# One kernel, the same pieces of work: another hand-fixed order, and other engines where a piece may choose

## The chip, the cores and the metric

The kernel runs on one core of one Trainium2 chip. A core has five instruction streams: PE (TensorE: matrix multiplications and transposes through the array), DVE (VectorE), ACT (ScalarE), POOL (GpSimd) and SP (SyncE, which here only issues DMAs). Each stream runs its instructions strictly in the order in which the program gives them; across streams only semaphores order things. The metric is the device time of one execution in microseconds (us), and the median of several runs is compared.

## The reference

Pooled attention (8 batches, 8 heads, 576 queries, 72 pooled keys) feeds a block with a rotation, a mixing over tokens and a gated channel layer:

```
k_p, v_p = mean of k, v over groups of 8 tokens          # 576 -> 72
attn     = softmax(q @ k_p.T / sqrt(64))
x        = (attn @ v_p), heads side by side              # [8, 576, 512]
theta    = x @ w_theta
zr, zi   = x * cos(theta), x * sin(theta)
y        = w_tok_r @ zr + w_tok_i @ zi                   # over the 576 tokens
u        = x + y
out      = u + relu(u @ w_ch)
```

## The kernel before

The work is cut into named pieces, each a Python generator that issues a few instructions and yields. A text constant, SCHEDULE, lists 2275 words; each word advances one piece by one step, and so the words fix the order of the instructions on every engine and of the DMAs on SP. A word may end in a letter, `a`, `v` or `g`: it says on which engine (ACT, DVE or POOL) this step does its copy or its elementwise operation. 698 of the words carry a letter; the others have no choice.

The loop that runs it:

```
    for word in SCHEDULE.split():
        name, engine = (word[:-1], word[-1]) if word[-1] in "vga" else (word, None)
        now[0] = engine
        next(streams[name])
```

The pieces, with b the batch, m one of five tiles of tokens (four of 128, one of 64), c one of four blocks of 128 channels and hf a half of the tokens (256 or 320 columns):

- `h0` to `h3`, `c0` to `c3`: load and convert `w_theta` and `w_ch`; `w` and `W`: the same for the token weights, which are also transposed on PE. They run once, in the first part.
- `k`, `v` (DMA), `K`, `V`, `Q`: load, pool and lay out keys, values and queries. In batch 0 the pooling of keys runs on PE (`K0.0`, line 610, tile kpp), and the queries are transposed on PE (tile pq, line 672) and copied out (tile qT).
- `S{b}.{m}`: scores on PE (lines 756 and 764, tile s), softmax on DVE, ACT and one of DVE and POOL (tile en, line 826; POOL's half instructions are line 199). From batch 2 on, the result goes through DRAM and back (DMAs `sh<-G` and `eraw<-sh`) and `E{b}` splits it into parts (tiles eh, er, eraw).
- `X{b}.{g}.{c}`: attention output on PE (line 974, tile pv), copied to x (tiles xa, xb).
- `T{b}.{m}`: split of x, three terms of theta on PE (line 1001, tile pt), sine and cosine on ACT, products on DVE into z.
- `Z{b}.{c}`: split of z into a high and a low part (tiles zh, zl); `M{b}.{c}.{hf}`: the mixing on PE, three terms of nine matmuls (line 1101, tile py), the sum on DVE (line 1107), a cast to uh (lines 214 or 216) and the rest ul (line 1114 on DVE, line 199 on POOL).
- `F{b}.{c}.{hf}`: three terms of four matmuls (line 1129, tile pf), relu and sum on DVE (line 1134), a transpose and four DMAs out.
- `D`: 24 matmuls on a constant that keep PE busy (tile warm).

Results of PE land in PSUM tiles that are used in turn: two buffers "mm" that M, F and a few others share, and single ones "th" (theta, some transposes), "px", "av", "tp" and "s". A piece that opens such a buffer waits until the reader of its last content is through. Almost everything is computed in pairs of a high and a low part, which is why each product has three terms.

Of the kernel before, what the change touches and what calls it, by code (L numbers as in the profile page):

```python
# [35 lines left out]
w0.1v X0.0.3v w1.0 S0.2 S0.2v X0.0.2 h3g w0.1 w0.1 S0.3 S0.3 K1.1g X0.0.2v S0.4g h3 h3a S0.4g S0.4 S0.4a S0.4 w0.1v
S0.3 S0.4v X0.0.0 h3 w1.0 w1.0a X0.0.0a W0 w1.0v w1.0 w1.0 w2.0 w2.0 w2.0a w2.0v w2.0 k1.0 W0a W0 S0.3g w3.1 S0.3g
S0.3 S0.3a S0.3 S0.3a X0.0.1 w1.0g w2.0 w2.1 X0.0.1a w1.1 T0.0a X0.2.3 K1.0v w1.1 w1.1v w1.1a w1.1 w1.1 T0.1a W0 W0a
W0 T0.0g T0.0 w2.1 w1.1v w2.1a w2.1a w2.1 T0.0 w2.1 X0.2.0 X0.2.0a T0.0 T0.0 T0.0 T0.0 W1 W1v w2.1g w4.0 w3.0 w3.0
w2.0v X0.2.2 X0.2.3a Q1.1 W1 T0.0 X0.2.1 X0.2.1a v1.2 X0.2.2v Q1.0 Q1.0 W1 W1a w3.0v W1 w3.1 T0.1v w3.1a w3.1v w3.1  # L40
# [5 lines left out]
c1 c1 c1 c1v M0.0.1 M0.0.1 S1.0 Z0.1v M0.0.1 M0.0.0 S1.0 S1.0v S1.1 S1.0g c1a V1g V1 M0.0.1 c2 M0.0.0 c1v c2 S1.1 c2v
c2 M0.0.0 c2 c2 M0.1.1 S1.0 S1.1 S1.0v S1.0 S1.0 S1.1 S1.1v M0.1.1 M0.1.0 S1.0a S1.0 M0.1.0 Z0.3a c2g c2a M0.1.1
M0.1.1 c2v S1.1g S1.1 S1.1a S1.1 S1.1 S1.1a S1.1 V1g c3 c3 V1g M0.1.0 M0.1.0 S1.2 S1.2 X1.0.3 X1.0.3v M0.3.0 Z0.2g
M0.2.0 M0.2.0 Z0.2v c3a c3 M0.2.0 c3 c3 c3v c3v M0.3.0 S1.2 X1.0.2 M0.0.0a S1.2 S1.2g S1.3 X1.0.2a X1.0.1 c3v X1.0.1a
S1.2v S1.2 S1.3 S1.3 M0.2.0 X1.0.0 S1.2v S1.2 X1.0.0v M0.2.1 M0.2.1 k2.1 K2.1v S1.2 S1.2a S1.3 S1.4 S1.4 Z0.3g M0.3.0  # L50
# [5 lines left out]
T1.2 T1.2 T1.2 V2.1g T1.1 T1.1 k3.0 V2g T1.4v F0.2.0 F0.2.0 F0.2.0 F0.2.0 T1.1 F0.1.0 F0.1.0 F0.1.0 F0.2.0 T1.1 T1.1a
T1.1 T1.1 T1.1 V2g F0.1.0 F0.2.0 F0.1.0 F0.1.0 T1.4 T1.4 T1.4 S2.0 S2.0 T1.4 T1.4 T1.4 T1.4 F0.0.0 K3.0g F0.0.0
M0.2.1v F0.0.0 F0.0.0 T1.3g T1.3v T1.3 T1.3 S2.0v S2.0v T1.3 M0.0.1g M0.3.1v V2 M0.3.1g T1.4 T1.4 T1.3 T1.3 S2.1 k3.1
F0.0.1 F0.0.1 Q3.0 M0.1.1g F0.0.1 K3.1g T1.3 F0.0.0 F0.0.0 T1.3 T1.3a T1.3 V2g S2.1 F0.0.1 V2g T1.3 T1.3 S2.0 S2.0
S2.1 F0.2.1 S2.1 F0.2.1 v3.0 F0.1.1 F0.1.1 F0.2.1 F0.2.1 Z1.0a F0.1.1 F0.1.1 S2.1g S2.1g Z1.0g S2.2 S2.2 K3 v3.2 S2.1  # L60
S2.2 F0.3.1 S2.2 S2.2g S2.1 F0.3.1 F0.3.1 F0.3.1 Z1.1a S2.2v Z1.1g S2.3 S2.3 E2.0 S2.2 S2.3 S2.3 F0.3.1 M1.0.0 M1.0.0
M1.0.0 M1.0.0 M1.0.0a M1.0.0g E2.0 E2.0a E2.0a S2.3v S2.3g F0.3.0 V3.2g S2.4 E2.0g E2.0g F0.3.0 K3a S2.3 Q3.0 Q3.1
S2.4 S2.4 M1.0.1 M1.0.1 M1.0.1 M1.0.1 S2.3 M1.0.1a M1.1.1 M1.1.1 M1.1.1 M1.1.1 M1.1.0 M1.1.0 X2.0.2 S2.4 S2.4v S2.4g
S2.4 S2.2 S2.4 Z1.3a Z1.3g M1.3.0 X2.0.2a M1.0.1g F0.1.1 X2.0.1 X2.0.1a M1.1.1g Q3.1 K3 K3a V3.0g k4.2 X2.0.0 X2.0.0v
X2.0.3 X2.0.3a T2.1a T2.1g S3.2 S3.2 T2.0a T2.0v M1.1.0 S3.2 S3.2 M1.1.0 E2.2 E2.2 E2.2 Z1.2a T2.0 F0.1.1 v3.1 T2.0
T2.0 T2.0 F0.3.1 M1.3.0 M1.3.0 T2.0 T2.0 Z1.2g S3.2v M1.3.0 T2.0 S3.2v S3.2 T2.0a M1.1.0v T2.1 T2.1 T2.0 T2.0 E2.2a
S3.3 S3.3 E2.2a S3.2 M1.3.0g T2.0 M1.3.0g E2.2g E2.2v M1.3.1 M1.3.1 M1.3.1 F0.2.1 S3.4 F0.2.1 K4.2g M1.3.1 X2.2.0 S3.3
S3.3 S3.3g T2.1 F0.0.1 T2.1 X2.2.1 X2.2.1a S3.3v S3.4 S3.4 S3.3 S3.4 F0.0.1 M1.2.1 M1.2.1 M1.2.1 M1.2.1 X2.2.3 X2.2.0a
S3.4v V3.1g S3.4g S3.4 X2.2.2 V3a V3g X2.2.3a S3.3 v4.2 X2.2.2a T2.2a S3.0 S3.0 E3.2 S3.0 T2.1 T2.2v M1.1.1g M1.3.1a
M1.3.1g S3.0 M1.2.1a S3.4 M1.2.0 M1.2.0 M1.2.1v M1.2.0 M1.2.0 F1.3.1 F1.3.1 F1.3.1 F1.3.1 V3 V3v S3.0g S3.0g S3.0 E3.2  # L70
# [1195 lines left out]
```

## Time and profile before

| what | value |
| --- | --- |
| runs shown, median | 605.32 us (604.28 to 607.11, three runs) |
| the profiled execution: its own time | 605.31 us |
| the profiled execution: its span, first to last instruction | 603.5 us |
| mean granted TensorE clock | 0.997 |
| PE busy | 577.2 us (96%) |
| DVE, ACT, POOL busy | 457.4, 329.5, 362.6 us |

The difference between the time and the span is 1.8 us around the first and the last instruction. Busy time counts the stretches in which at least one instruction of the engine ran; matmuls are pipelined, so one that is listed with 300 ns can follow the one before it after 120 ns.

### The profile page before, as it was taken

What the parts mean: (1) busy time and instruction counts of PE and PEld (TensorE: products, weight loads), DVE (VectorE), ACT (ScalarE), POOL (GpSimd) and SP (SyncE); (2) the same over time, 40 slices, a digit from 0 to 9 for tenths busy, and PEclk for the clock granted to TensorE, in tenths of its full rate; (3) what the DMA queues carried; (4) which work ended last, traced back from release to release, by engine and by line L of the source; (5) the groups of instructions that cost most, each with busy time, mean ns of one, the idle gap of its engine ahead of it and who ended that gap; (6) DMA issues with size and microseconds to landing.
All of it is one profiled execution on the core that took longest, in us unless ns stands there. A gap on an engine that the chain in (4) does not pass through costs nothing.

```text
span 603.5 us, 11700 instructions
## 1 busy us (share of the span) xinstructions
PE 577.2 (96%) x4072; PEld 537.8 (89%) x4072; DVE 457.4 (76%) x840; ACT 329.5 (55%) x701; POOL 362.6 (60%) x513
## 2 busy tenths in 40 slices
PE   4889979989999999999999998999999999999996
...
GB/s 243 206 171 262 75 79 71 73 133 85 144 126 179 124 116 131 105 155 102 96 163 82 180 72 170 85 115 65 112 120 105 98 27 10 105 14 26 12 30 90
DMA packets 176987, 65.73 MB, mean 109 GB/s; under 512 B 147744, under 2 KB 162080, under 8 KB 176928
## 3 DMA queue, kind: packets, MB, share of 16 engines
...
HBM read 46.66 MB, written 18.28 MB: 108 GB/s over the span
## 4 chain that ended last, share of the span: by engine, by line
PE 86%; DVE 7%; ACT 4%; issue 1%; DMA 1%; SPq 0%; DVEq 0%; ACTq 0%
PE py L1101 37%; PE pf L1129 16%; PE pt L1001 15%; PE pv L974 6%; PE s L764 5%; PE px L1044 2%; DMA kpst<-in_k_dram 1%; PE kpp L610 1%; PE wt L476 1%; PE s L756 1%; ACT zh L214 1%; PE ths L430 1%; DVE ul L1114 0%; ACT g L1052 0%; PE pq L672 0%
## 5 line engine op out<-in xcount | busy, mean ns | idle before, releaser
L1101 PE MATMUL py<-WTh,zh 128*128 128x256 f32 (+1 forms) x576 | 87.8, 298 | 3.6 <-ACT zh L214 3.6
L1101 PE MATMUL py<-WTl,zh 128*128 128x256 f32 (+1 forms) x576 | 86.9, 294 | 0.0
L1101 PE MATMUL py<-WTh,zl 128*128 128x256 f32 (+1 forms) x576 | 86.2, 296 | 0.0
L1101 PEld LDWEIGHTS py<-WTh,zh 128*128 128x128 f32 x576 | 80.7, 190 | 4.8 <-ACT zh L214 4.2
L1101 PEld LDWEIGHTS py<-WTl,zh 128*128 128x128 f32 x576 | 79.7, 188 | 0.2
L1101 PEld LDWEIGHTS py<-WTh,zl 128*128 128x128 f32 x576 | 79.1, 189 | 0.6
L199 POOL TENSOR_TENSOR en<-e_eps,ri 128x256 f32<-128x256 f32 (+3 forms) x72 | 42.1, 606 | 48.0 <-DVE ri L823 40.6
L199 POOL TENSOR_TENSOR zl<-z,zh 128x384 fp32r<-128x384 f32 (+1 forms) x64 | 51.2, 833 | 8.1 <-ACT zh L214 4.9
L1005 ACT ACTIVATE g<-pt,c_magic 128x512 f32<-128x512 f32 x35 | 24.1, 688 | 45.1 <-PE pt L1001 41.1
L1129 PE MATMUL pf<-uh,chh 128*128 128x320 f32 (+1 forms) x256 | 45.3, 299 | 1.6 <-DVE xb L1107 1.6
L1129 PE MATMUL pf<-uh,chl 128*128 128x320 f32 (+1 forms) x256 | 45.0, 297 | 0.0
L1129 PE MATMUL pf<-ul,chh 128*128 128x320 f32 (+1 forms) x256 | 44.0, 295 | 0.0
L1007 DVE SCALAR_TENSOR_TENSOR g<-g,pt 128x512 f32<-128x512 f32 x35 | 23.8, 681 | 25.6 <-ACT g L1005 25.6
L1001 PE MATMUL pt<-th,xh 128*128 128x512 f32 x148 | 41.6, 403 | 0.9 <-ACT qT L214 0.8
L1001 PE MATMUL pt<-th,xl 128*128 128x512 f32 x148 | 40.3, 394 | 0.0
L764 PE MATMUL s<-kpT,qT 128*128 128x144 f32 x256 | 37.2, 288 | 3.2 <-DVE qT L216 1.9
L1129 PEld LDWEIGHTS pf<-uh,chh 128*128 128x128 f32 x256 | 37.6, 188 | 2.9 <-DVE xb L1107 1.9
L1001 PE MATMUL pt<-tl,xh 128*128 128x512 f32 x148 | 40.1, 393 | 0.0
L764 PEld LDWEIGHTS s<-kpT,qT 128*128 128x128 f32 x256 | 33.9, 189 | 4.3 <-DVE WTl L487 1.5
L1129 PEld LDWEIGHTS pf<-ul,chh 128*128 128x128 f32 x256 | 37.4, 188 | 0.2
L1129 PEld LDWEIGHTS pf<-uh,chl 128*128 128x128 f32 x256 | 37.1, 188 | 0.1
L819 ACT ACTIVATE e_eps<-e_eps 128x576 f32<-128x576 f32 (+1 forms) x30 | 20.6, 686 | 29.5 <-DVE e_eps L815 29.3
...
## 6 DMA issues: line engine op xcount, KB each, us to landing
...
```

The lines of the kernel that those rows point to most:

```text
L199: nc.gpsimd.tensor_tensor(out[:, r], a[:, r], b[:, r], op)
L214: nc.scalar.copy(out, src)
L430: nc.tensor.matmul(sum_, ident, t, start=True, stop=False)
L764: nc.tensor.matmul(scs[c // 2][:n, 2 * SP * (c % 2) : 2 * SP * (c % 2 + 1)], qT[:, c, t0 : t0 + n], kpT[:, c, :], start=True, stop=True,)
L819: nc.scalar.activation(e[:n], e[:n], AF.Exp, scale=scale)
L974: nc.tensor.matmul(pv[:, :gn], l, r, start=i == 0, stop=i == len(terms) - 1)
L1001: nc.tensor.matmul(pt, l[:, c, :], r[:, c, :], start=i == 0, stop=i == 11)
L1005: nc.scalar.activation(g, pt, AF.Identity, bias=c_magic)
L1007: nc.vector.scalar_tensor_tensor(g, g, MAGIC, pt, ALU.subtract, ALU.subtract)
L1044: nc.tensor.transpose(px[:, P * c : P * c + P], x[:, c], ident)
L1101: nc.tensor.matmul(py[:, :n], l[:, kk, :], r[:, kw, t], start=i == 0, stop=i == 3 * NK - 1)
L1129: nc.tensor.matmul(pv[:, :n], l[:, kk, o], uhl[r][:, kk, t], start=i == 0, stop=i == 11)
```

## The change

Only SCHEDULE differs. It has the same 2275 words if the letters are taken off, each as often as before, so every piece issues what it issued. They stand in another order, and 226 of the 698 letters differ: 58 steps go from DVE to POOL and 58 from POOL to DVE, 32 from DVE to ACT and 31 from ACT to DVE, 26 from ACT to POOL and 21 from POOL to ACT. In sum ACT has 231 of these steps (235 before), POOL 257 (252), DVE 210 (211). Of the 702 steps that use PE, 194 keep their place in PE's order, 584 are at most three places from it, 673 at most eight, and none is more than 21 away.

The diff, cut to the stretches that matter below (the order of the start; the fourth and fifth tile of theta of batch 0; the end of the mixing of batch 0; scores and attention of batch 6):

```
-Q0.4 Q0.4 Q0.4a h0 h0 h0a h0v h0 h0 h0v k0.0 K0.0 h0 h0v h0 h2 h2 k0.1 K0.0a K0.1 Q0.0 Q0.0 K0.1v Q0.0a K0 K0a k0.2
-K0.2 K0.2v h1 h2a K0 K0v S0.0 S0.0 Q0.1 Q0.1 Q0.1v S0.1 h1 h1v h1v S0.0 S0.0 h2g h2 h2 h2g h1 Q0.3 Q0.3 S0.1 S0.1 h1
-h1g D S0.0 S0.0g S0.0g Q0.3a Q0.2 S0.1 Q0.2 Q0.2v S0.2 S0.2 S0.2 h1 h2 S0.0 h1v h1 v0.1 S0.1 S0.1v S0.1v S0.1 h3 k1.2
...
-W3 T0.1 T0.1 T0.1 T0.3 Q1.2 Q1.2 T0.3 Q1.3 Q1.3 T0.2 T0.2 T0.4g w4.0g W3 W3a W3 T0.2a T0.2 T0.2 T0.3 Q1.2v V1.0g c0
-T0.4v T0.3 T0.3 W4 W4a W4 Q1.3a T0.2 W4a W4 c0 c0a c0 c0 T0.3 T0.3 c0 T0.4 T0.4 T0.4 T0.4 T0.4 T0.4 V1.2g V1g W2 W2a
...
-M0.2.1 M0.3.1 M0.3.1 Q2.0 Q2.0 S1.4 S1.4a S1.4 S1.4 S1.4a T1.0 T1.0 S1.4 X1.2.2 M0.2.0v M0.2.0v M0.2.1 k2.0 K2.0g K2
-T1.0 T1.0 T1.0 X1.2.2a X1.2.0 K2a X1.2.0a k2.2 K2.2g M0.1.0g M0.1.0v F0.3.0 v2.0 M0.3.0g X1.2.3 X1.2.3a V2.0v T1.0 K2
...
-M4.2.1 S6.1 T5.3v T5.3 M4.2.1 M4.3.0a F4.1.0 S6.0 M4.2.1 M4.2.1v S6.0 V6 Q7.0 T5.3 T5.3 T5.3 T5.3 T5.3 F4.1.0 M4.3.0g
...
-F4.0.1 F4.3.0 K7a E6.0g E6.0v E6.0g S6.4 S6.4g S6.4g X6.0.1 X6.0.0 X6.0.1v M5.0.1 M5.0.1 X6.0.0a Q7.1 S6.3 M5.0.1a
...
+h0 h0 h0a h0v h0 k0.0 K0.0 K0.0a h0 h0g h0 h0a h0 h2 h2 h2g h2v h2 k0.1 K0.1 K0.1a K0 K0a Q0.0 Q0.0 Q0.0v k0.2 K0.2
+K0.2v K0 K0v h1 h1 h1a h1v S0.0 S0.0 S0.0 S0.0 Q0.1 Q0.1 Q0.1v Q0.2 S0.1 h1 h1 h1g Q0.2 Q0.2v S0.1 S0.1 S0.1 k1.2 Q0.3
+K1.2g h2 h2g S0.0 D Q0.4 Q0.4 Q0.4v S0.2 S0.2 S0.0v S0.0v Q0.3 Q0.3v S0.2 S0.1 h1 h3 h3 h1v S0.2 S0.0 S0.0v S0.0 S0.0v
+h3v h3v h2 h3 v0.1 S0.1g S0.1g S0.1 S0.1a v0.0 S0.1 S0.1a h3 h3v S0.2 h1 S0.4 S0.4 h2a h2 w0.0 w0.0 w0.0a w0.0v w0.0
...
+Q1.3 Q1.3a W3 Q1.2 Q1.2 T0.3 T0.3 W3 T0.1 X0.2.3g T0.1 T0.2a w4.0g W3a W3 V1.2g Q1.2v T0.3 T0.2 T0.2 T0.2 T0.3 T0.4a
+T0.3 T0.4v W4 W4a W4 c0 c0 c0a c0 c0 c0 c0g c0g T0.3 W4a W4 T0.4 T0.4 T0.3 T0.3a T0.4 T0.4 T0.4 T0.3 V1a T0.3 c0g Q1.4
...
+S1.1 S1.1a S1.1 S1.1 S1.1a c3 c3a S1.2 S1.2 V1g S1.1 Z0.3g M0.1.0 M0.1.0 M0.3.0 M0.3.0 V1g X1.0.3 c3 c3 c3 c3v Z0.2v
...
+M0.3.1 M0.0.0a k2.0 Q2.0 K2.0g S1.4 S1.4v S1.4g S1.4 M0.2.1a S1.3 M0.1.0a M0.2.0g S1.4v S1.4 S1.4 S1.4a S1.4 T1.0 T1.0
+T1.0 k2.2 F0.3.0 X1.2.2 X1.2.2a K2 K2a X1.2.0 X1.2.0a F0.3.0 K2.2g K2 K2a M0.3.0v T1.1v X1.2.3 X1.2.3a T1.0 T1.0 T1.0a
+M0.2.0v M0.0.0g v2.0 M0.1.0v F0.3.0 X1.2.1 V2.0v M0.3.1 X1.2.1v T1.2v T1.2v T1.2 T1.2 T1.0 T1.0 M0.3.1 T1.0 Q2.1 Q2.1
...
+v7.2 M4.2.1 M4.2.1 M4.2.1 M4.2.1 M4.2.1v T5.3 T5.3 M4.0.0g T5.3 F4.1.0 T5.3 F4.1.0 S6.1 M4.3.0v M4.2.1g T5.3 F4.0.0
...
+F4.3.0 S6.4 F4.1.1 F4.1.1 S6.3g V6g Q7.0 M5.1.0 M5.1.0 M5.1.0 S6.4 M5.1.0 K7a F4.0.1 F4.0.1 E6.0g E6.0a E6.0v E6.0g
+F4.0.1 S6.3 F4.0.1 Q7.1 V7.1g M5.0.1 M5.0.1 S6.4 S6.4 F4.1.0 M5.0.1 S6.4v S6.4v S6.4 X6.0.1 X6.0.1a Z5.2v F4.1.0 Z5.2g
```

## Rows read from the trace of the kernel before

**Rows 1.** The page: TensorE's busy time; TensorE in 40 slices of the span, in tenths.

```profile
PE 577.2 (96%) x4072; PEld 537.8 (89%) x4072; DVE 457.4 (76%) x840; ACT 329.5 (55%) x701; POOL 362.6 (60%) x513
...
PE   4889979989999999999999998999999999999996
```

**Rows 2.** Busy time by stretch: stretch, its us, PE, PEld, DVE, ACT, POOL, clock, DMA.

```profile
0.00:20.00 20.00, 11.26 (x74) 9.54 (x75) 8.64 (x18) 7.20 (x14) 6.29 (x13) 1.00 0.89 245
...
40.00:60.00 20.00, 19.14 (x98) 11.97 (x96) 18.95 (x34) 17.89 (x44) 10.56 (x14) 1.00 0.88 228
...
80.00:100.00 20.00, 16.59 (x109) 15.65 (x108) 17.75 (x33) 17.84 (x57) 6.89 (x10) 0.91 0.19 60
...
150.00:200.00 50.00, 50.00 (x371) 47.61 (x371) 43.29 (x82) 31.46 (x51) 42.40 (x61) 1.00 0.66 145
...
590.00:603.50 13.50, 8.42 (x66) 8.21 (x64) 5.81 (x13) 0.00 (x0) 0.00 (x0) 0.99 0.58 94
```

**Rows 3.** What TensorE waited for: us in total, times, longest us.

```profile
PE pq L672 <- DMA qst<-in_q_dram: 4.2, 1, 4.2
PE py L1101 <- ACT zh L214: 3.6, 3, 2.1
PE kpp L610 <- DMA kpst<-in_k_dram: 3.5, 1, 3.5
PE s L764 <- DVE qT L216: 1.9, 2, 1.0
PE pf L1129 <- DVE xb L1107: 1.6, 1, 1.6
...
PE pt L1001 <- ACT qT L214: 0.8, 1, 0.8
PE kpp L610 <- ACT kp L214: 0.7, 1, 0.7
...
PE pv L974 <- DVE er L882: 0.5, 1, 0.5
```

**Rows 4.** TensorE in order of time, start: start, us, instruction, [idle before, releaser].

```profile
8.33 3.78 PE L610 MATMUL kpp<-kpst,ident 128*128 128x128 f32 x16 [3.52 <-DMA kpst<-in_k_dram]
...
14.23 2.05 PE L610 MATMUL kpp<-z,ident 128*128 128x128 f32 x16 [0.68 <-ACT kp L214]
...
27.14 1.22 PE L764 MATMUL s<-kpT,qT 128*128 128x144 f32 x8 [0.87 <-DVE qT L216]
```

**Rows 5.** SP's DMA issues in order of time, the start.

```profile
0.74 0.72 SPq L665 DMA_DIRECT2D qst<-in_q_dram  x1
1.52 0.60 SPq L408 DMA_DIRECT2D WTh_st<-in_moe_w_theta_dram  x1
```

**Rows 6.** ScalarE in order of time, 13 to 14.2 us.

```profile
13.36 0.67 ACT L379 ACTIVATE WTh_st<-WTh_st 128x512 f32<-128x512 f32 x1 [5.16 <-PE ths L430]
13.92 0.25 ACT L214 COPY kp<-kpp 128x128 f32<-128x128 f32 x1
```

**Rows 7.** Groups of one shape on GpSimd: count, busy us, mean ns, idle before.

```profile
L199 POOL TENSOR_TENSOR en<-e_eps,ri 128x256 f32<-128x256 f32 x40 | 26.0, 671 | 29.8 <-DVE ri L823 24.0 <-PE s L756 3.6 <-ACT xb L978 1.3
```

**Rows 8.** The same view on VectorE.

```profile
L826 DVE TENSOR_TENSOR en<-e_eps,ri 128x512 f32<-128x512 f32 x10 | 8.4, 840 | 0.2
```

**Rows 9.** VectorE in order of time, 129.8 to 133.3 us.

```profile
129.78 3.01 DVE L1114 TENSOR_TENSOR ul<-xa,uh 128x256 fp32r<-128x256 f32 x1
132.81 0.49 DVE L1107 TENSOR_TENSOR xb<-py,xb 128x320 f32<-128x320 f32 x1
```

**Rows 10.** Line 1114 on VectorE: ns min/median/max, first and last start, forms.

```profile
L1114 DVE TENSOR_TENSOR ul<-xa,uh x15: 410/426/3009, 129.8 to 568.4; 128x256 fp32r<-128x256 f32 x15
```

**Rows 11.** VectorE in order of time, near 441 us (batch 6).

```profile
440.24 0.86 DVE L940 TENSOR_TENSOR er<-eraw,er 32x256 fp32r<-32x256 f32 x2
```

**Rows 12.** TensorE in order of time, near 441 us (batch 6).

```profile
441.08 0.28 PE L974 MATMUL pv<-eh,Vh 128*128 128x256 f32 x1
```

**Rows 13.** The chain that ended last, 480 to 560 us: start, us, what.

```profile
480.90 2.76 PE pt L1001 x12
...
488.18 1.41 PE pf L1129 x12
```

More of the change, by code (lines that the diff above doesn't have):

```diff
@@ L36 @@
[L36 to L40, printed above, removed]
@@ L46 @@
[L46 to L50, printed above, removed]
@@ L56 @@
[L56 to L70, printed above, removed]
@@ new lines @@
+X1.2.3a k3.2 K3.2g M0.1.1g M0.3.1a T1.2 F0.3.0 F0.2.0 T1.2 T1.2 v2.1 V2.1g V2g V2g V2 T1.2 T1.2 T1.2a S2.0 S2.0 v3.2
+F0.2.0 F0.2.0 T1.2 T1.3v T1.1 T1.1 T1.1 T1.3g T1.2 T1.2 k3.0 K3.0g T1.1 F0.2.0 F0.2.0 T1.1 F0.2.0 F0.1.1 F0.1.1 T1.4a
+T1.4v T1.1 T1.1 V2g T1.1a T1.1 T1.1 F0.1.0 F0.1.0 F0.1.0 F0.1.0 F0.1.0 F0.3.0 F0.3.0 T1.4 T1.1 S2.0 S2.0 k3.1 T1.4
+T1.4 T1.4 T1.4 T1.4 T1.4 T1.4 F0.1.0 F0.0.0 F0.0.0 F0.0.0 F0.0.0 F0.0.0 T1.3 T1.3 T1.3 S2.0g S2.0v S2.0 S2.1 M0.0.1g
+M0.3.1g F0.0.0 M0.2.1g S2.0 F0.0.1 F0.0.1 V3.2g T1.4 T1.3 T1.3 T1.3 T1.3 T1.3a T1.3 Q3.0 S2.1 F0.1.1 T1.3 F0.0.1
@@ new lines @@
+F0.0.1 S2.2 T1.3 F0.2.1 F0.2.1 F0.2.1 F0.1.1 F0.0.1 F0.0.1 S2.1 S2.1 F0.2.1 K3.1g S2.1g S2.1v F0.3.1 Z1.0a Z1.0g
+F0.3.1 S2.2 S2.2 S2.1 M1.0.0 S2.1 K3 S2.2 F0.3.1 F0.3.1 Z1.1a S2.2g S2.2v M1.0.0 S2.3 S2.3 S2.3 Z1.1g S2.2 V2g M1.0.0
+E2.0 M1.0.0 M1.0.0a S2.3 M1.0.1 M1.0.1 S2.4 Q3.0 F0.1.1 S2.3g S2.3v E2.0 M1.0.1 M1.0.1 E2.0a M1.1.1 M1.1.1 v3.0 M1.1.1
+E2.0a E2.0g E2.0v X2.0.1 Q3.1 S2.4 S2.4 K3v X2.0.1v V3.0g S2.2 M1.1.1 S2.3 M1.1.0 S2.4 S2.4g S2.4g S2.3 X2.0.2 X2.0.2a
+M1.1.1a M1.1.1g K3 K3a X2.0.3 X2.0.0 M1.1.0 Q3.1 S2.4 M1.1.0 M1.1.0 M1.1.0g k4.2 Z1.3a Z1.3g X2.0.3a X2.0.0a T2.0a
@@ new lines @@
+T2.0v E2.2 S2.4 S3.2 S3.2 E2.2 E2.2 T2.1a T2.1v Z1.2a Z1.2g T2.0 T2.0 F0.3.1 F0.3.1 T2.0 T2.0 S3.2 T2.0 T2.0 T2.0
+M1.3.0 M1.3.0 S3.2 S3.2v M1.3.0 S3.2v S3.2 S3.2 M1.3.0 T2.0a S3.3 S3.3 K4.2g T2.0 M1.0.0g T2.0 T2.0 E2.2a E2.2a S3.3
+M1.3.1 M1.3.1 M1.0.1a M1.3.1 E2.2g E2.2v M1.0.1g F0.2.1 S3.3 S3.3g M1.3.1 S3.3v v3.1 V3.1g F0.1.1 T2.1 T2.1 T2.1
+M1.3.0a M1.3.0g S3.4 S3.4 X2.2.3 X2.2.2 X2.2.2v F0.2.1 S3.3 S3.3 M1.2.1 M1.2.1 X2.2.3a X2.2.1 S3.4 S3.4 S3.4v X2.2.0
+M1.2.1 X2.2.0a V3g M1.2.1 E3.2 X2.2.1a M1.2.1a V3g S3.4v S3.4 S3.4 k4.0 M1.2.1g T2.1 S3.0 S3.0 M1.3.1a T2.1 M1.3.1g V3
@@ new lines @@
+T2.3v T2.3 F1.2.0 F1.2.0 T2.4g S3.1g T2.4 T2.4 T2.3 T2.3 T2.4 T2.4 S3.1 S3.1 T2.4 K4.1g F1.0.0 F1.0.0 F1.0.0 E3.0
+F1.0.0 T2.4 T2.4 T2.4v T2.4 T2.4 F1.3.0 T2.4 k5.0 F1.3.0 Z2.1a K4 K4a T3.2a E3.0 F1.3.0 F1.3.0 F1.3.0 F1.1.0 F1.1.0
+F1.1.0 F1.1.0 F1.1.0 F1.1.0 Z2.1v Q4.0 E3.0a E3.0g E3.0v E3.0g M2.1.0 M2.1.0 M2.1.0 M2.1.0 M2.1.0g Z2.0a Z2.0v M2.1.1
+M2.1.1 M2.1.1 M2.0.0 Q4.1 M2.0.0 M2.0.0 T2.4 T2.4 M2.0.0 K4 F1.0.0 Q4.1 Z2.2g Z2.2g X3.0.2 X3.0.2a K5.0v X3.0.3
+X3.0.3v K4a M2.0.1 M2.0.1 M2.0.1 M2.0.1 M2.0.1g v4.1 M2.1.1 M2.1.0g X3.0.0 X3.0.1 X3.0.0v S4.0 S4.0 X3.0.1a T3.1g
@@ new lines @@
+M2.2.1 T3.2v T3.1v T3.1 k5.2 K5.2v T3.1 S4.0 T3.0g Z2.3a S4.0 T3.1 M2.2.1 M2.2.1 T3.0g M2.3.0 T3.1 T3.1 T3.1 T3.1
+T3.1a S4.0g S4.0v S4.0 T3.1 M2.3.0 Z2.3g T3.1 T3.1 T3.0 T3.0 T3.0 T3.0 M2.2.1 M2.2.1a Q5.0 S4.0 T3.3v T3.3g T3.0
+M2.1.1g v4.2 S4.1 S4.1 V4.1g T3.0 F1.3.0 T3.0 T3.0a M2.2.0 M2.2.0 M2.2.0 v4.0 M2.2.0 T3.0 T3.0 T3.0 T3.3 T3.3 T3.3
+E4.0 V4.2g S4.1 S4.1 S4.1v S4.1v T3.3 T3.3 M2.0.0v M2.0.0g S4.1 S4.1 V4.0g T3.3 S4.2 S4.2 T3.3 T3.3a T3.3 T3.3 T3.3
+M2.2.1v M2.3.0 M2.2.0g M2.2.0g M2.3.0 S4.2 S4.2 M2.3.0v M2.0.1v F1.0.0 M2.3.1 M2.3.1 M2.3.1 M2.3.1 M2.3.0g M2.3.1g
@@ new lines @@
+M2.3.1g T3.2 T3.2 T3.2 E4.0 F2.2.0 F2.2.0 T3.2 F2.2.0 T3.2 T3.2 F2.2.0 F2.2.0 S4.2g T3.2 k5.1 S4.2g F2.0.0 F2.0.0
+F2.0.0 F2.0.0 F2.2.0 M2.1.1v F2.0.0 F2.0.0 F2.2.1 F2.2.1 F2.2.1 F2.2.1 V4a V4g K5.1g F2.0.1 F2.0.1 F2.0.1 T3.2a T3.2
+E4.0a E4.0a T3.2 F2.0.1 T3.2 Z3.0a Z3.0g S4.3 S4.3 S4.3 F2.1.0 E4.0g F2.1.0 F2.1.0 F2.1.0 F2.1.0 F2.1.0 E4.0v F2.3.1
+F2.3.1 F2.3.1 F2.3.1 K5 S4.4 K5a v5.1 Q5.0 V4 V4g V4g S4.3 S4.2 F2.3.0 F2.3.0 F2.3.0 F2.3.0 S4.3v S4.3v F2.3.0 M3.0.0
+M3.0.0 K5 Z3.1a V5.1g M3.0.0 M3.0.0 Q5.1 S4.3 S4.3 F2.3.1 F2.1.1 F2.1.1 F2.1.1 F2.1.1 X4.0.1 X4.0.1a S4.4 F2.3.1 S4.4
@@ new lines @@
+S4.4 X4.0.2 M3.0.1 M3.0.1 Z3.1g X4.0.2v F2.3.0 S4.4g M3.0.1 S4.4g M3.0.1 F2.2.1 Q5.1 X4.0.3 M3.0.0a F2.0.1 X4.0.0
+X4.0.0a X4.0.3a T4.1a v5.0 M3.1.0 M3.1.0 v5.2 T4.0a T4.0v K5a S4.2 S5.2 S5.2 Z3.3a Z3.3g M3.1.0 S4.4 M3.1.0 M3.1.0a
+V5.0v S4.4 M3.1.1 M3.1.1 M3.0.0v M3.1.1 S5.2 T4.0 T4.0 T4.0 T4.0 Z3.2v Z3.2g M3.1.1 S5.2 T4.0 S5.2v S5.2g V5.2v T4.0
+T4.0 T4.0a T4.0 M3.3.0 M3.3.0 T4.0 T4.1v T4.1 E4.2 E4.2 M3.3.0 E4.2 E4.2a F2.2.1 E4.2g E4.2g M3.3.0 M3.3.0a S5.3 S5.3
+M3.0.1a S5.3 v6.1 Q6.0 S5.2 T4.0 F2.1.1 F2.1.1 T4.1 T4.1 k6.2 M3.2.1 M3.2.1 F2.0.1 E4.2g M3.2.1 X4.2.3 S5.3 X4.2.3a
```

151 lines of the change are left out of this document (69 added, 82 removed).

## The prediction

> **What bounds the kernel now.** I read the page first. TensorE is busy for 577.2 of 603.5 us, and its row of 40 slices has digits under 9 among the first nine slices (to about 136 us), once near 370 us, and in the last slice [rows 1]. The table by stretch says the same in us: of the first 20 us TensorE uses 11.3, from 80 to 100 us 16.6, but from 150 to 200 us all 50, and the last 13.5 us hold 8.4 [rows 2]. So there are three parts. From 150 us to the last matmul the kernel is bound by TensorE's own work, which the change leaves as it is. The tail of 13.50 - 8.42 = 5.1 us after the last matmul is relu, transpose and the DMAs out of the last piece; both orders end with a final of 256 columns whose last step carries v, so the tail stays. What an order can win is TensorE's idle time, 603.5 - 577.2 = 26.3 us, less the tail: 21.2 us. The list of TensorE's waits says what ended the larger pieces of it: the first load of keys 3.5, the first queries 4.2, the split z of a batch 3.6 in three waits, and single waits of 0.5 to 1.9 us for copies on VectorE and ScalarE [rows 3]. Most of them lie before 150 us.
>
> **The change part by part.** The pieces are the same, so no engine's work changes but by the letters. I count those at nothing: in sum ACT loses 4 steps, POOL gains 5 and DVE loses 1, and the work is in cover: after 150 us TensorE has no idle time while VectorE is busy for 43.3 of 50 us and POOL for 42.4 [rows 2]. Without that cover one step moved from DVE to POOL would cost, for the largest kind that moves often, 2 x 0.67 - 0.84 = 0.5 us [rows 7, 8]. Most moves of TensorE's pieces are at most three places; I cost them at nothing too where the trace shows no wait near them, because TensorE then only does the same pieces in turn. That leaves the waits the new order touches; the minus signs are gains.
>
> *First load of keys.* Before, SP issues the queries of tile 4 first and starts on the weights at 1.52 instead of 0.74 us [rows 5]; the keys come behind and land when TensorE's wait ends at 8.33 [rows 4]. The new order begins with the weights and moves `Q0.4` (one DMA, four transposes, one copy) to between the warm-up `D` and `S0.2`. All that follows on SP is issued 0.78 us earlier. A load may be held by the bytes ahead of it as well as by its issue, which no row here separates, so the gain lies between 0 and 0.8; I take 0.6, near the issue.
>
> *Second block of keys.* `K0.1` waited 0.68 us for the copy kp [rows 4], a 0.25 us copy that stood on ScalarE behind a 0.67 us step of `h2`, which itself had waited for the matmuls of `h0` [rows 6]. In the new order the copy stands ahead of both. Gain 0.7, or 0 if the second load of keys lands no earlier.
>
> *Scores of tile 2.* `S0.2` waited 0.87 us for the copy of its queries [rows 4]. Now the warm-up and `Q0.4` stand between `Q0.2` and `S0.2`, so the copy is covered: 0.9. The softmax of tile 1 takes it back: its normalisation moves from DVE to POOL (two POOL instructions of 0.67 in place of one of 0.84 [rows 7, 8]), and tile 0's goes to DVE ahead of it along with a copy of queries; I charge 0.9, so these two cancel, with bounds of 0.9 either way. The start sums to -0.6 - 0.7 = -1.3 us.
>
> *Theta of tile 4.* `T0.4` waited 0.8 us for a copy qT [rows 3]: `Q1.3` held the buffer "th", and its copy stood on ScalarE behind six other steps. Now `Q1.3a` is the next word after `Q1.3`, with `Q1.2`, two theta terms and `W4` before `T0.4`. Gain 0.8, at least 0.
>
> *First attention of batch 1.* `X1.0.3` waited 0.5 us for er [rows 3]. Two terms of `M0.3.0` now stand ahead of it, more than that: gain 0.5, at least 0.
>
> *First final of batch 0.* `F0.3.0` waited 1.6 us for a PSUM buffer [rows 3], since the sum on VectorE that frees it (0.49 us) stood behind an ul of 3.01 us [rows 9]; the same instruction has a median of 0.426 [rows 10]. In the new order that ul (`M0.2.0v`, its second step) comes after the first two terms of `F0.3.0`, and the sum of `M0.2.1` comes well before. Gain 1.6; nothing, if the casts to uh, one of which is now on POOL behind the pooling of `K2.0`, hold it as long.
>
> The Trainium skill, page "SBUF — State Buffer", section "Who interferes with whom", says that a VectorE instruction with two SBUF inputs and a GpSimd one that reads SBUF exclude each other for the whole instruction, and which one waits is a matter of issue order. By it the 3.01 us in [rows 9] is a wait for POOL's train of instructions, and will come again wherever such an ul meets one; in the new order the third term of `F0.3.0` needs an ul that stands on VectorE behind this one, and the gain of 1.6 would be lost.
>
> *What gets tighter.* The first waits of M for z (3.6 us in three [rows 3]) stay: the distance from the last theta of a batch to its first M is about the same in both orders. In the first groups of batches 2, 5, 6 and 7, fewer of TensorE's pieces now lie between the last scores and the attention output that uses them. For batch 6 three theta terms (2.76 us) and two terms of a 256-column F (2/3 of 1.41, 0.94) leave, and a term of M leaves as another enters: 3.7 us less cover [rows 13]. There the attention began at 441.08, and the er that it needs was done at 440.24 + 0.86 = 441.10, just in time for the last of its four terms [rows 11, 12]. If the chain of softmax, DRAM and E comes as much earlier relative to TensorE, this costs nothing; if not at all, up to 3.7 us. Each of its instructions has moved too, and the words of `E6.0` now stand several of TensorE's steps ahead of `X6.0.1`, where before three of them stood right in front of it. I take 1.0 in all, nearer the lower end, and 3.7 for one group as the upper one.
>
> Sum: -1.3 - 0.8 - 0.5 - 1.6 + 1.0 = -3.2 us. The profiled execution took 605.31 us (span 603.5 and 1.8 around it), equal to the median of 605.32, so the forecast is 605.3 - 3.2 = 602.1 us.
>
> **The rivals.** About 0.5%, 3.0 us, is what a measurement of this kernel can tell from no change: below 602.3 counts as faster, above 608.3 as slower.
>
> *The early gains run into the next bound.* From 40 to 60 us VectorE is busy for 18.95 and ScalarE for 17.89 of 20 us [rows 2], so an earlier start may only make TensorE wait there for the same copies, and end in the same wait for the first split z (the three sum to 3.6 us, the longest is 2.1 [rows 3]). Against it: the waits of TensorE between are short ones. Then the 1.3 and 0.8 are lost: 605.3 - 0.5 - 1.6 + 1.0 = 604.2 us.
>
> *The block of 3 us stays in front of the first final.* Then 602.1 + 1.6 = 603.7 us. For it speaks that POOL's pooling of keys stands close to it in both orders; against it, that at least half of the 15 such instructions took no more than 0.426 us [rows 10]. The rule of the page "SBUF — State Buffer" of the Trainium skill would give this case.
>
> *Attention comes late: slower.* In those four groups the chain doesn't move with TensorE's order and each stands for 3.7 us. It decides from a sum of 4.2 + 3.0 = 7.2 us on, two full groups. With three: 605.3 - 4.2 + 11.1 = 612.2 us. For it: no slack in batch 6 [rows 11, 12]. Against: TensorE's list of waits has only the 0.5 us of batch 1 for such an input [rows 3].
>
> *More of the waits go.* If the start keeps its full gain (-0.8 - 0.7 - 0.9 = -2.4), the three later gains hold (-2.9), nothing new waits, and half of the 3.6 us for z goes too (-1.8): 605.3 - 7.1 = 598.2 us.
>
> **How the numbers follow.** Chances: the forecast 0.45, with its own range 600.0 to 604.0, split 0.27 below 602.3 and 0.18 above; the next bound 0.20; the block 0.07; late attention 0.13; more waits gone 0.15. The predicted time is 602.1 us. Faster: 0.27 + 0.15 = 0.42; within 0.5%: 0.18 + 0.20 + 0.07 - 0.02 = 0.43, the 0.02 for starts that lose more than they win; slower: 0.13 + 0.02 = 0.15. The range reaches down to 597.5, just under the last rival, and up to 608.0, where nothing is gained and one group comes late by 2.7 of its 3.7 us; beyond it lie most of the late attention and, below, a little of the last rival.
>
> **What would show it.** In the changed profile: the keys land before 8.0 us and the second kpp follows without a wait for kp; no waits of pt for qT, of pv for er in batch 1, and of pf for xb; the first M still waiting for zh; TensorE busy for all of 150 to 550 us; a tail of 5.1 us. It is wrong if pv waits for eh, er or eraw in batches 2 to 7, if TensorE's idle time up to 150 us is no smaller, or if pf waits near 130 us for ul or uh.

## The result and the profile after

The changed kernel takes 599.39 us (median of four executions, 598.61 to 600.73) against 605.32 us; the ratio is 0.9901 with a 95% interval of 0.9872 to 0.9931. It is faster by 1.0%. Forecast was 602.1 us, 3.2 us less than the profiled execution of before; the gain is nearly twice that. The profiled execution of after took 600.73 us, the longest of the four, with a span of 598.9 us, 4.6 less than before.

The page of after: busy time of TensorE, TensorE in 40 slices of the span, and its granted clock in tenths.

```profile
PE 578.3 (97%) x4072; PEld 539.4 (90%) x4072; DVE 453.7 (76%) x840; ACT 321.8 (54%) x691; POOL 369.4 (62%) x529
...
PE   5899979999999999999999999999999999999997
...
PEclk9999979999999999999999999999999999999999
```

Only slices 1, 2, 6 and the last are under 9 now, where [rows 1] have seven. The clock row has a dip of its own in slice 6, and it will matter. Busy time by stretch, after (columns as in [rows 2]):

```profile
80.00:100.00 20.00, 17.17 (x107) 16.75 (x107) 16.48 (x28) 15.86 (x58) 7.76 (x11) 0.83 0.20 63
100.00:150.00 50.00, 49.83 (x357) 45.96 (x356) 41.81 (x85) 39.63 (x121) 32.94 (x53) 1.00 0.53 101
...
200.00:250.00 50.00, 48.59 (x342) 46.12 (x341) 37.79 (x67) 27.09 (x48) 35.02 (x47) 1.00 0.57 121
```

From 80 to 100 us TensorE is busier than before, 17.17 against 16.59, yet at a granted clock of 0.83 instead of 0.91 [rows 2]: part of that busy time is slow work. From 100 to 150 us it is nearly full (49.83 of 50). From 200 to 250 us 1.4 us are idle. What TensorE waited for, after:

```profile
PE kpp L611 <- DMA kpst<-in_k_dram: 6.7, 1, 6.7
PE s L765 <- DVE WTl L488: 1.7, 1, 1.7
PE py L1102 <- ACT zh L215: 1.4, 2, 1.2
PE pv L975 <- POOL eraw L200: 1.2, 1, 1.2
PE s L765 <- DVE qT L217: 1.0, 1, 1.0
PE py L1102 <- DVE zh L217: 0.8, 1, 0.8
PE per L869 <- DVE Vr L690: 0.7, 1, 0.7
PE pe L861 <- DVE qT L217: 0.7, 1, 0.7
```

Against [rows 3]: pq's 4.2 and kpp's 3.5 us have become one wait of 6.7; the waits of pf for xb, of pt for qT, of kpp for kp and of pv for er are gone; z costs 2.2 us instead of 3.6. New are pv's wait for eraw and some shorter ones, and the scores wait 1.7 us for WTl, where [rows 3] leave out a wait of 1.3.

To see where the 4.6 us came from, I laid the two traces side by side by TensorE's work: matmul by matmul in order of their ends, each counted with the median step of its kind. The median step stands for a matmul that waits for nothing, so idle time and slow clock shift one trace against the other. Where pieces have swapped places, as around 20 us of work, the figure also moves by over 1 us within a few us of work and says little by itself. At equal work the new order leads by 1.1 us after 20 us of work, 2.8 after 25, 2.4 after 40, 3.3 after 60, 4.3 after 62 (the first mixing matmul, at 84.50 instead of 88.37), only 2.6 after 70, 3.0 after 105, 4.6 after 110 (`F0.3.0`), 3.5 after 200 (the wait for eraw) and 3.7 at the last matmul. The last 0.85 us come in the tail: 5.10 us before, 4.25 after.

### The profile page after: what moved, and what is told of

Read it like the earlier page. It is cut to its first block, busy times and chain, and to the rows that moved or that the text cites. A ratio compares the mean times of both kernels' runs of the same rounds, so it can differ in the third digit from the quotient of the medians.

```text
span 598.9 us, 11680 instructions
## 1 busy us (share of the span) xinstructions
PE 578.3 (97%) x4072; PEld 539.4 (90%) x4072; DVE 453.7 (76%) x840; ACT 321.8 (54%) x691; POOL 369.4 (62%) x529
## 4 chain that ended last, share of the span: by engine, by line
PE 89%; DVE 4%; ACT 2%; DMA 2%; POOL 2%; issue 1%; SPq 0%; DVEq 0%; POOLq 0%
PE py L1102 38%; PE pt L1002 15%; PE pf L1130 15%; PE pv L975 7%; PE s L765 5%; PE px L1045 2%; DMA kpst<-in_k_dram 2%; PE kpp L611 1%; PE s L757 1%; PE vpp L611 1%; PE pe L861 1%; PE ths L431 1%; DMA eraw<-sh 1%; POOL eraw L200 1%; DVE WTl L488 0%
## 5 line engine op out<-in xcount | busy, mean ns | idle before, releaser
L200 POOL TENSOR_TENSOR zl<-z,zh 128x384 fp32r<-128x384 f32 (+1 forms) x84 | 69.5, 859 | 22.7 <-DVE zh L217 17.3
L200 POOL TENSOR_TENSOR en<-e_eps,ri 128x256 f32<-128x256 f32 (+3 forms) x66 | 37.6, 592 | 20.0 <-DVE ri L824 19.1
L799 DVE TENSOR_REDUCE mx<-s 128x8 f32<-128x576 f32 (+2 forms) x42 | 30.0, 718 | 8.2 <-PE s L765 5.4
```

The lines of the kernel that those rows point to most:

```text
L200: nc.gpsimd.tensor_tensor(out[:, r], a[:, r], b[:, r], op)
L799: nc.vector.tensor_reduce(mxv, scv, AX.X, ALU.max)
```

## The experiments

Theory A: the gain is a sum of waits that went, and each is kept to the end. Theory B: an early lead is used up by the next bound. Theory C: the letters, not the order, make the gain. The rest are theories about single places.

**The new order up to a point, then the words of before.** Four kernels, cut where both orders have done all but one or two of the same words:

```
-SCHEDULE = words of before
+SCHEDULE = first n words of the new order, then the words of before that are left, in their order
 n = 121 (c_start), 310 (c_theta), 443 (c_mix0), 956 (c_b3)
```

> The new order and letters up to 23.7 us of TensorE work, then the words of before. Theory A (the gain is a sum of waits that went, each kept to the end): at this point the traces have the new order 1.1 to 2.8 us ahead at equal TensorE work, so 602.5 to 604.2 us, and the waits behind it stay as in before. Theory B (a lead is used up by the next bound, the stretch in which VectorE and ScalarE are nearly full, and by the wait for the first zh): 605.3 us, with a longer wait for zh than the 2.1 us of before.

> The new order up to 55.7 us of TensorE work (the third step of W4), then the words of before. Theory A: the lead there is 3.0 us, so 602.3 us, with the first wait for zh near the 2.1 us of before. Theory B: the first wait for zh grows by what was won, and the time is 604.5 us or more.

> The new order up to 86.6 us of TensorE work, the most part of the mixing of batch 0, then the words of before. Theory A: the lead there is 3.2 us, so 602.1 us; pf still waits 1.6 us for its buffer near 130 us. Theory B: under 1 us of gain.

> The new order up to 199.9 us of TensorE work, in front of the attention of batch 3 that waits in the new kernel, then the words of before. Theory A: the lead there is 4.6 us and nothing behind it is lost, so 600.7 us, with a tail of 5.1 us and no wait of pv for eraw. Theory B: the attention of batch 3 waits in this kernel too, and 601.9 us or more come out.

Measured, beside before at 605.94 us (28 executions):

| kernel | median us | range | ratio (95%) |
| --- | --- | --- | --- |
| c_start | 607.56 | 606.21 to 610.25 | 1.0015 (0.9999 to 1.0032) |
| c_theta | 604.36 | 602.11 to 607.55 | 0.9979 (0.9961 to 0.9997) |
| c_mix0 | 600.39 | 600.16 to 600.65 | 0.9905 (0.9879 to 0.9930) |
| c_b3 | 603.15 | 601.40 to 605.59 | 0.9959 (0.9940 to 0.9979) |

The new start alone brings nothing, although its profile has the keys in at 6.27 us. Its wait for zh is 2.1 us as in before, so theory B's way of losing the lead is wrong too. The profile of c_start from 36 to 48 us shows where it went (columns as in [rows 2]; clock third from the end):

```profile
36.00:40.00 4.00, 2.52 (x11) 1.12 (x9) 4.00 (x10) 3.38 (x15) 2.80 (x4) 1.00 0.46 152
40.00:44.00 4.00, 4.00 (x12) 1.90 (x12) 1.96 (x7) 2.12 (x10) 1.74 (x4) 0.57 1.02 381
44.00:48.00 4.00, 4.00 (x16) 2.70 (x16) 2.38 (x5) 1.82 (x5) 1.30 (x2) 0.50 0.46 136
```

TensorE is busy for 2.52 of 4 us, with a wait of 1.5 us of pv for xa in it, and then the granted clock falls to 0.50, that is to 1.2 GHz; the same matmuls then take longer. The lead at equal work goes from 1.7 us after 30 us of work to a lag of 1.4 us after 35. Two of the other three splices have a stretch at 1.2 GHz there in their profile as well, c_theta none. c_b3 and c_mix0 have the same words up to 86.6 us of work, and still differ by 2.1 us at 35 us of it, before their words part. So these four sort out less than they were meant to: c_mix0 comes out over 1 us under A: the words up to 86.6 us of work can give as much as the whole change. c_theta comes out near B's time (604.36 us, where B gave 604.5 or more), but its first wait for zh is 2.1 us, as A said; what it loses, it loses at the scores of batch 1, which wait 2.9 us for WTl, where before has 1.3. c_b3, profiled in an execution of 604.8 us, has the 0.8 us wait of pv for eraw that B gave it, but most of its loss is the stretch at 1.2 GHz: 2.5 us ahead at 30 us of work, level at 35.

One expectation for c_mix0 failed, and it matters for the first final: pf does not wait 1.6 us for its buffer but 0.4, although the words there are those of before. VectorE, GpSimd and TensorE in c_mix0:

```profile
125.29 1.80 DVE L216 CAST uh<-xa 128x256 fp32r<-128x256 f32 x1
127.12 0.42 DVE L1114 TENSOR_TENSOR ul<-xa,uh 128x256 fp32r<-128x256 f32 x1
```

```profile
126.09 0.84 POOL L216 CAST uh<-xb 128x320 fp32r<-128x320 f32 x2
```

```profile
128.10 0.72 PE L1129 MATMUL pf<-uh,chh 128*128 128x256 f32 x4 [0.40 <-DVE xb L1107]
```

Here GpSimd's train ends at 126.09 + 0.84 = 126.93. The cast in front of the ul is the one held beside it (1.80 us; the same cast takes 0.40 in sum_first at 130.36), and the ul, which took 3.01 us in [rows 9], comes after the train and takes 0.42. The same words thus have the long ul or not, by where VectorE stands against GpSimd's train.

**Order without letters, letters without order.**

```
 order_only:   the words of after, each with the letter that it has in before
 letters_only: the words of before, each with the letter that it has in after
```

> The new order with every letter as before. Theory A (the order does it; the letters cost and bring nothing): within 1 us of the changed kernel, 598.5 to 600.5 us. Theory C (the letters make it): 603 us or more, with waits where an engine has become late.

> The order of before with the new letters. Theory A: within 1 us of before, 604.3 to 606.3 us. Theory C: 602 us or less.

Measured: 661.45 us (1.0907, 1.0880 to 1.0933) and 678.34 us (1.1193, 1.1166 to 1.1221). A and C both fall: neither half has a worth of its own, and each without the other costs 55 to 72 us. One place of order_only shows how. In the changed kernel the ul of `M6.2.0` is a step with g; here it carries v as in before. TensorE, then VectorE, near 595 us of order_only:

```profile
597.60 0.79 PE L1130 MATMUL pf<-ul,chh 128*128 128x256 f32 x2 [3.96 <-DVE ul L1115]
```

```profile
595.11 0.69 DVE L1056 TENSOR_TENSOR z<-px,sn 128x512 f32<-128x512 f32 x1 [0.69 <-ACT sn L1049]
596.53 0.69 DVE L1058 TENSOR_TENSOR z<-px,g 128x512 f32<-128x512 f32 x1 [0.72 <-ACT g L1053]
597.13 0.41 DVE L1115 TENSOR_TENSOR ul<-xa,uh 128x256 fp32r<-128x256 f32 x1
```

The ul takes 0.41 us, but it stands on VectorE behind two products that wait for sine and cosine, and TensorE stands still for 3.96 us. Over the whole kernel TensorE is idle for 57.0 us instead of after's 20.6 and busy for 602.7 instead of 578.3, at a mean clock of 0.967. A letter cost here not its duration but the queue in which its step landed.

**One word moved by one place.** The sum of `M0.2.1` ahead of the ul of 3.01 us [rows 9]:

```
-X1.2.2 M0.2.0v M0.2.0v M0.2.1 k2.0
+X1.2.2 M0.2.0v M0.2.1 M0.2.0v k2.0
```

> Before, with one word moved by one place: VectorE's sum of M0.2.1 ahead of the ul of M0.2.0 that took 3.01 us. Theory A (the wait of F0.3.0 comes from that place alone): pf no longer waits 1.6 us, 603.7 us. Rival D (the long ul only moves the wait, to the third term of F0.3.0 or to the next piece that needs it): 605.3 us, and TensorE waits elsewhere between 130 and 140 us.

Measured: 605.13 us against 606.02, ratio 0.9990 (0.9971 to 1.0009); the times alone cannot tell the two kernels apart. In the profile the wait of pf is gone, but the long ul is there again. VectorE, then GpSimd, then TensorE in this kernel:

```profile
131.20 3.00 DVE L1114 TENSOR_TENSOR ul<-xa,uh 128x256 fp32r<-128x256 f32 x1
```

```profile
130.95 0.39 POOL L216 CAST uh<-xa 128x256 fp32r<-128x256 f32 x1
131.31 1.42 POOL L199 TENSOR_TENSOR ul<-xa,uh 128x256 fp32r<-128x256 f32 x2
132.68 1.24 POOL L216 CAST uh<-xb 128x320 fp32r<-128x320 f32 x3
```

```profile
137.51 1.20 PE L1001 MATMUL pt<-th,xh 128*128 128x512 f32 x4 [0.63 <-DVE xh L216]
```

GpSimd's train runs without a gap up to 132.68 + 1.24 = 133.92, and the ul that began in it ends 0.3 us later, at 134.20. VectorE is late behind it, and TensorE then waits 0.63 us for a cast xh. At equal work 0.8 of the 1.6 us stay won in this pair of profiles. Both theories were half right.

**Two words of F6.2.1 earlier.** Its transpose and its four DMAs on SP:

```
-Z7.0v F6.2.0 ... F7.0.1v F6.2.1 F6.2.1 F7.1.1
+Z7.0v F6.2.1 F6.2.1 F6.2.0 ... F7.0.1v F7.1.1
```

> Before, with the last two words of F6.2.1 (its transpose and its four DMAs on SP) at the end of its own work instead of among the last finals. Theory E (those four DMAs keep SP's queue two DMAs behind ScalarE's to the end): tail 4.25 instead of 5.1 us, 604.5 us. Rival F (the tail differs from one execution to the next): a tail of 5.1 us.

Measured: 604.85 us against 606.02, ratio 0.9981 (0.9959 to 1.0002); the interval reaches just over 1, so the time alone does not show a gain. The profile fell on the longest execution (610.07 us); its tail is 4.23 us. SP's issues at the end of before, then of this kernel, then of after:

```profile
589.57 2.33 SPq L1145 DMA_DIRECT2D out_dram<-R  x4
592.02 9.34 SPq L1145 DMA_DIRECT2D out_dram<-z  x14
```

```profile
594.26 11.54 SPq L1145 DMA_DIRECT2D out_dram<-z  x16
```

```profile
587.90 8.57 SPq L1146 DMA_DIRECT2D out_dram<-z  x12
```

Before, the last transposition ends at 598.92 + 0.45 = 599.37 and SP's last issue at 592.02 + 9.34 = 601.36, 2.0 us later; after, 595.19 + 0.45 = 595.64 and 587.90 + 8.57 = 596.47, 0.8 us later. In f6_early the last transposition ends at 604.52 + 0.45 = 604.97 and the last issue at 594.26 + 11.54 = 605.80, also 0.8 us later: SP's queue is no longer behind. The tail is 5.09 to 5.41 us in all four splices, which end as before, and 4.23 to 4.30 in every kernel that ends without these DMAs: theory E, not chance.

**The changed kernel again, and one letter of it altered.** In after, all steps of `E3.2` but one are GpSimd's; e32_v gives one of them to VectorE:

```
 after_again: the changed kernel
 e32_v:  -E3.2g S3.1 F1.3.1   (the subtraction of er)
         +E3.2v S3.1 F1.3.1
```

> The changed kernel itself, unchanged, in more executions, beside those of before. If its 599.4 us is typical: 598.6 to 600.7, ratio 0.988 to 0.993. If its few executions fell on few stretches at the half clock, as the spread of 601.4 to 605.6 us of the kernel spliced at 199.9 us lets one suspect: 601 to 603 us, the slow ones with a second stretch at 1.2 GHz near 41 us.

> The changed kernel with one letter altered: the subtraction of er of E3.2 on VectorE instead of GpSimd. Theory G (the 1.2 us wait of pv for eraw at 218 us stands at the end of a train of three GpSimd steps): GpSimd's last step starts about 1.8 us earlier, the wait is gone, 1.2 us less than the changed kernel. Rival H (VectorE holds up a final in its place): no gain, and pf waits for VectorE near 213 to 217 us.

Measured beside before at 606.16 us: after_again 599.81 us (599.52 to 604.20, ratio 0.9908, 0.9880 to 0.9936); e32_v 601.06 us (598.66 to 603.17, 0.9918, 0.9892 to 0.9943). The result stands. The profile of after_again, an execution of 599.99 us, has a granted clock of 0.61 from 40 to 44 us and 0.97 from 44 to 48, where c_start has 0.57 and 0.50: the stretch at 1.2 GHz can befall the changed kernel too, shorter here, and at equal work it cost about 1.6 us against after, which has none there. One of the six executions took 604.2 us; it was not profiled, so its cause is not known.

The letter brings nothing that can be seen: the two ranges overlap. First TensorE and GpSimd in after at 218 us:

```profile
218.22 0.41 PE L975 MATMUL pv<-eraw,Vh 128*128 128x320 f32 x1 [1.18 <-POOL eraw L200]
```

```profile
211.85 1.26 POOL L217 CAST eh<-eraw 128x1280 fp32r<-128x1280 f32 x1 [2.31 <-DMA eraw<-sh]
213.19 1.82 POOL L200 TENSOR_TENSOR er<-eraw,er 32x320 fp32r<-32x320 f32 x2
215.09 3.08 POOL L200 TENSOR_TENSOR eraw<-eraw,eh 128x640 fp32r<-128x640 f32 x2
```

Then GpSimd, VectorE, ScalarE and TensorE in e32_v:

```profile
212.40 3.33 POOL L200 TENSOR_TENSOR eraw<-eraw,eh 128x640 fp32r<-128x640 f32 x2
```

```profile
212.47 3.60 DVE L941 TENSOR_TENSOR er<-eraw,er 32x320 fp32r<-32x320 f32 x2
216.10 0.49 DVE L1135 SCALAR_TENSOR_TENSOR xb<-pf,xb 128x320 f32<-128x320 f32 x1
```

```profile
218.88 0.77 ACT L979 ACTIVATE xb<-pv 128x320 f32<-128x320 f32 x2 [1.56 <-DVE R L1141]
219.37 0.42 PE L975 MATMUL pv<-eh,Vh 128*128 128x320 f32 x1 [1.67 <-ACT xb L979]
```

GpSimd is done 2.4 us earlier (215.73 instead of 218.17; 0.8 of it because its train starts that much earlier, at 211.06 instead of 211.85) and pv does not wait for eraw. But VectorE's two subtractions, 0.86 us for a pair of 256 columns in [rows 11], take 3.60 beside GpSimd's train, and what stands behind them on VectorE is late: the final's sum (216.10) and its transpose R, ScalarE's copy of x, which waits 1.56 us for that transpose, and with the copy the next pv, by 1.67 us. H was right that VectorE loses what GpSimd wins, but the place is pv, not pf.

**TensorE's gaps ahead of the mixing filled.** Eleven matmuls on the constant into a PSUM buffer that is free (the trace lists each as two, as it does the twelve of `D`, which stand as 24 above):

```
+    def fill():
+        p = bank([P, 512], "th", "fill")
+        for n in 6, 5:
+            for _ in range(n):
+                nc.tensor.matmul(p[:, 0:P], ident, ident, start=True, stop=True)
+            yield
-K1 K1a S1.0 Z0.0a M0.0.0
+K1 D2 K1a S1.0 Z0.0a D2 M0.0.0
```

> The changed kernel with eleven more matmuls on the constant, six ahead of the first scores of batch 1 and five ahead of the first matmul of the mixing, where TensorE waited 1.66 and 1.17 us. Theory J (the clock falls to 1.2 GHz at 83.5 us because TensorE is idle there): no stretch at 1.2 GHz behind them; TensorE wins half of the 5.9 us from the first mixing matmul (84.50) to the end of the stretch (90.36), 2.9 us, less 0.3 for matmuls that come in the way: 2.6 us less than the changed kernel. Rival K (the clock falls whatever stands in these gaps): the stretch stays, no gain or 0.3 us more.

> Both edits in one kernel. By theories G and J together 3.8 us less than the changed kernel, about 595.6 us; by J alone 2.6 less, by G alone 1.2 less, by the rivals H and K the time of the changed kernel.

Measured: fill 597.28 us (596.35 to 597.62), ratio 0.9855 (0.9831 to 0.9879), 2.5 us under after_again; fill_e32 598.28 us (597.73 to 600.02), 0.9875 (0.9854 to 0.9896). Theory J's direction is shown: with both gaps filled, no stretch at 1.2 GHz stands behind them. Its size is less sure than 2.5 against 2.6 us looks. At equal work, between 62 and 70 us, fill wins 2.6 us over after but 1.6 over after_again; and the profile of fill also lacks the stretch near 41 us and the wait of pv for eraw that after_again has, which the filling, as far as the traces show, has nothing to do with. The altered letter costs 1.0 us here. TensorE in after, then in fill:

```profile
82.03 1.30 PE L765 MATMUL s<-kpT,qT 128*128 128x144 f32 x8 [1.66 <-DVE WTl L488]
84.50 2.29 PE L1102 MATMUL py<-WTh,zh 128*128 128x256 f32 x9 [1.17 <-ACT zh L215]
```

```profile
80.19 1.60 PE L320 MATMUL fill<-ident 128*128 128x128 f32 x12 [0.30 <-DVE g L1015]
81.64 1.22 PE L772 MATMUL s<-kpT,qT 128*128 128x144 f32 x8
82.69 1.28 PE L320 MATMUL fill<-ident 128*128 128x128 f32 x10
84.02 1.33 PE L1109 MATMUL py<-WTh,zh 128*128 128x256 f32 x9
```

The same nine matmuls take 2.29 us after two idle gaps and 1.33 after two filled ones. Busy time and clock from 84 to 92 us, after, then fill:

```profile
84.00:88.00 4.00, 3.50 (x16) 3.51 (x17) 3.36 (x6) 3.94 (x10) 0.47 (x1) 0.50 0.02 4
88.00:92.00 4.00, 4.00 (x24) 4.00 (x23) 1.40 (x3) 2.38 (x14) 0.00 (x0) 0.71 0.49 164
```

```profile
84.00:88.00 4.00, 3.98 (x32) 3.98 (x33) 3.73 (x7) 3.94 (x13) 0.00 (x0) 1.00 0.00 0
88.00:92.00 4.00, 4.00 (x30) 4.00 (x29) 3.77 (x7) 3.89 (x18) 1.21 (x2) 1.00 0.52 164
```

Both stretches of after look full by busy share; only the clock and the number of matmuls (16 and 24 against 32 and 30) show what was lost. fill is the fastest kernel of this study.

## Why the prediction was right, and where its sizes were off

The direction holds and the time lies inside the range, just under the forecast's own range of 600.0 to 604.0 and nearer to the rival "more of the waits go" (598.2 us, chance 0.15) than to the forecast. Most of the signs it named came: the keys before 8.0 us, the second kpp without its wait, no waits of pt, er and xb, the first M waiting for zh. The tail did not stay, TensorE was not busy for all of 150 to 550 us (2.2 us of waits), and one of its signs of being wrong came true: pv waits for eraw in batch 3.

That the sum came no further off is partly luck. It left out gains of 0.9 us (a wait of pe), about 1.0 (the first wait for zh) and 0.85 (the tail), and on the other side 1.7 us of slow clock. It also took the 150 to 200 us of [rows 2] for all that follows: before has 2.1 us of waits behind 150 us, 1.6 of them for zh. By its terms, in the profiled executions:

- **First load of keys**, forecast 0.6 with bounds 0 and 0.8: mis-sized. The keys were in at 6.71 us instead of 8.33; ten profiles with the new start have 6.25 to 6.71 (mean 6.45), four with the old 8.09 to 8.37 (mean 8.24). I looked at the issue of the first weights only. SP's issues of the keys, before and after:

```profile
2.17 0.43 SPq L554 DMA_DIRECT2D kpst<-in_k_dram  x1
```

```profile
1.20 0.42 SPq L555 DMA_DIRECT2D kpst<-in_k_dram  x1
```

They moved by 0.97 us. The other 0.65 is about what the 128 KB of queries ahead of them would take at the 246 GB/s that the DMA view gives for before's first 9 us (0.53, an estimate); that it is the bytes was not tried. On the other side I forgot that TensorE had turned those queries inside its wait: between the 4.2 and the 3.5 us of waiting [rows 3, 4] lie 0.7 us of work that now come later. What is left of 1.62 is 0.96.
- **Second block of keys**, 0.7: right, the second kpp follows without a wait for kp. With the 1.0 above that makes 1.7. The first scores start 1.8 us sooner (16.97 instead of 18.77), and of that the transposes of tile 4 that are still to come take 0.4 (23.96 to 24.35): 1.4, near the 1.3 of the sum.
- **Scores of tile 2** against the softmax of tile 1, cancelling: the wait for qT went to pe (0.7), and per waits 0.7 for Vr. The 0.9 us wait of pe for the normalised tile, which I had not listed, went as well, so the lead is 2.8 us at 25 us of work and 2.0 at 30. The charge of 0.9 was too high.
- **Theta of tile 4**, 0.8, and **batch 1**, 0.5: both waits are gone. The first gave little, since wt now waits 0.45 us for WTl there; for the second the lead grows by 0.8 us between 80 and 90 us of work.
- **First final**, 1.6: about 1.5 us of lead between 105 and 110 us of work. The rival of the long block named the right danger: in sum_first it came back. It did not come here: VectorE does these uls from 127.8 to 129.5 us, none longer than 0.469, while GpSimd is idle from 127.1 to 133.1. But the order of these words, to which the prediction put the gain, is not needed for it: c_mix0 has those of before and its pf waits 0.4 us. The gain hangs on where VectorE stands against GpSimd's train.
- **z waits stay**: wrong. The first mixing matmul started 3.87 us earlier, and the first wait for zh fell from 2.08 to 1.17 us. TensorE in before, then in c_theta:

```profile
88.37 2.29 PE L1101 MATMUL py<-WTh,zh 128*128 128x256 f32 x9 [2.08 <-ACT zh L214]
```

```profile
85.66 2.29 PE L1101 MATMUL py<-WTh,zh 128*128 128x256 f32 x9 [2.08 <-ACT zh L214]
```

  Most of the 3.87 is lead from before this place: the last theta term ends at 78.33 instead of 82.65. What shortened the wait itself is the place of the channel weights `c0`. In before VectorE's three steps of them run from 82.31 to 84.19, right in front of theta's last rounding; in after at 77.47 to 79.33, and ScalarE's steps of `c0` are ahead as well. c_theta, spliced just in front of `c0`, ends its last theta term when after does (78.34) but has these steps at 79.59, in front of the last rounding; it waits 2.08 us for zh and starts the mixing 1.16 us later than after. Of the lead 1.7 us went again to a longer stretch at 1.2 GHz, which the prediction had no term for.
- **What gets tighter**, 1.0: the right size, 1.2 us, in the wrong place. No pv waits in batches 2, 5, 6 and 7; it is batch 3, whose letters I counted at nothing. The wait is not constant either: 0.6 us in after_again, none in fill, for a reason that I have not found.
- **Letters cost nothing**: true of the pair, and no more than that, as order_only and letters_only show.
- **The tail stays**: wrong by 0.85 us. I read the last piece and not what stands ahead of it in SP's queue.

The Trainium skill, page "SBUF — State Buffer", section "Who interferes with whom", says that a VectorE instruction with two SBUF inputs contends with a GpSimd one that reads SBUF, that the lock is exclusive, and that the issue order decides who waits. The traces agree on the contention, and show VectorE as the loser: 3.00 us for an ul whose median is 0.426 [rows 10], 3.60 for a pair of subtractions, each beside a GpSimd train without gaps, while GpSimd's own pair grew only from 3.08 to 3.33. The cast of 1.80 us in c_mix0, with one input, is held beside such a train too.

What stays open: why one execution of the same words has the stretch at 1.2 GHz near 41 us and another not. The Trainium skill, page "TensorE: Matmul & The Clock Gate", section "Part 1: The HAM clock gate (the "warmup" mystery)", says that the gate watches activity on a count that runs free of the kernel, so that the same code differs from run to run. c_mix0 and c_b3, and after and after_again, differ near 41 us with the same words, which fits; no run here tests it. This spread limits what the splices can tell to about 2 us each. How the 5.9 us divide over the stretches is therefore read from the traces at equal work, not from timed kernels; the tail, the final's wait and the clock were each tried alone, and of these only the clock's kernel, fill, stands clear of its neighbour in time.
